# Decay attention followed by a mixture of experts: weight pieces loaded from the first chunk, splits at other places, reciprocals per expert

## The chip, the cores and the metric

The kernel runs on one core of one Trainium2 chip. The metric is device time in microseconds (us), lower is better. Engine names in the profile: PE is TensorE, DVE is VectorE, ACT is ScalarE, POOL is GpSimd, SP is the sync engine, which only asks for transfers here.

## The reference

```
# decay attention: q, k, v are (2, 8, 768, 64), lam is (8), blocks of 64
for b in range(nb):
    intra = einsum('bhic,bhjc->bhij', qb, kb) * Dmask        # Dmask[i,j] = lam ** (i-j) for i >= j
    intra = einsum('bhij,bhjd->bhid', intra, vb)
    inter = einsum('bhid,bhde->bhie', qb * lam_pow, kv_state)
    out[block b] = intra + inter
    kv_state = lam_block * kv_state + einsum('bhsd,bhse->bhde', kb * rev_pow, vb)
# mixture of experts on x = (1536 tokens, 512): 8 experts, hidden 1024, capacity 384 tokens
expert = argmax(x @ w_gate); gate = softmax(x @ w_gate)[expert]
out[token] = gate * (relu(x[token] @ w1[expert]) @ w2[expert])   # 0 past the capacity
```

All data are float32.

## The kernel before

**Attention.** The 1536 tokens are cut into 12 chunks of 128 (six to a batch entry). For each chunk s two loads of 512 KB come from memory: q and k transposed (tile qk, called load(s, 0)) and k and v by rows (tile kv, load(s, 1)); four buffers hold each kind. The work on a chunk is spread over several turns of one loop: score(s+2) and mask(s+2) run two turns ahead, attend(s) and state(s) in turn s, turn(s-1), choose(s-1), rows(s-1) and soft(s-1) one turn behind, place(s-2), placed(s-2) and scatter(s-2) two behind. score is q times k on PE (L412); mask multiplies by the decay on DVE (L419); attend forms x (L431, and L439 with the decayed qd and the state); state forms the new state (L465 on PE, L471 or L473 on DVE). decay_k and decay_q make kd (L395) and qd (L387) on POOL. turn multiplies x by an identity and the gate weights at once (tile tp, L482), which gives rows of tokens and gate logits. choose picks the expert on DVE (oh at L503 is the one-hot choice, cum at L507 the running count). soft makes the sum of exponentials on ACT, weight its reciprocal on DVE. place multiplies by a triangle on PE (L527, L528) for the rank of each token within its expert, placed takes it out on DVE (pr, L536), and scatter writes the 128 rows of the chunk to their places in xs, a table in device memory, with one indirect DMA that POOL issues (L553). Each row of xs is 512 values, the gate weight and the token's number. Before the first scatter, fill (L337) writes zeros into the places of experts 0 and 1 by two plain DMAs.

**Weights.** Every expert has 8 pieces of 128 x 1024 float32 (512 KB; four of w1, four of w2). load_w asks for a piece (tile wraw, four buffers), split_hi makes its high half on ACT (whi, L105), split_lo the remainder on DVE (wlo, L113), and all products of the experts are made of three products of such halves. In the loop, the tables LOAD, HI and LO say in which turn which piece is loaded and split.

**Experts.** Expert 0 gets its first 128 tokens while the last scatters run (class Solo, object first: turn, rest, up, cross, down, finish) and its next 128 in second. This stretch is called the transition here. Experts 1 to 7 follow in one loop of 232 places each (L770, L778, L796, L805). Rows of an expert are read back from xs (load_rows), tokens_of makes the token numbers, and put writes 128 rows of the result by an indirect DMA from POOL (L175). overflow is only run when an expert has more tokens than places.

**Order.** The schedule is written by hand: every engine runs its instructions in the order in which they stand in the program, and waits for other engines by semaphores. SP asks for all big loads and POOL issues the indirect DMAs, so a wait in one of these queues holds whatever stands behind it.

Of the kernel before, what the change touches and what calls it, by code (L numbers as in the profile page):

```python
# [8 lines left out]
F32 = mybir.dt.float32  # L9
# [28 lines left out]
LOAD = {3: (0,), 4: (1,), 5: (2,), 6: (3,), 7: (4,), 8: (5,), 9: (6,), 10: (7,), 11: (8,)}  # L38
HI = {5: (0,), 6: (1,), 7: (2,), 8: (3,), 9: (4,), 10: (5,), 11: (6,)}
LO = {6: (0,), 7: (1,), 8: (2,), 9: (3,), 10: (4,), 11: (5,)}  # L40
# [3 lines left out]
def kernel(  # L44
# [94 lines left out]
    rw, wt, ti = {}, {}, {}  # L139

    def load_rows(e, t=None):
        if e >= E:
            return
        if e > 0:
            rw[e] = rw_p.tile([P, RS // 32, P], F32, tag="rw", name="rw")
            wt[e] = ti_p.tile([P, NTT, 2], F32, tag="wt", name="wt")
            ti[e] = ti_p.tile([P, NTT], I32, tag="ti", name="ti")
            for q in range(4):
                i = nc.sync.dma_start(
                    out=rw[e][32 * q:32 * q + 32],  # L150
                    in_=xs[e * STR:e * STR + RS, P * q:P * q + P].rearrange("(t p) c -> p t c", p=32),
                )
                tc.add_to_no_dep_group("rows", i.ins)
# [5 lines left out]
        if t == 0:  # L159
            rw[e] = rw_p.tile([P, NTT, ROW], F32, tag="rw", name="rw")  # L160
            wt[e] = rw[e][:, :, DM:DM + 2]
            ti[e] = ti_p.tile([P, NTT], I32, tag="ti", name="ti")
        i = nc.sync.dma_start(out=rw[e][:, t], in_=xs[t * P:t * P + P])
        tc.add_to_no_dep_group("rows", i.ins)

    def tokens_of(e, t=None):
# [4 lines left out]
        )  # L171

# [8 lines left out]
    class Solo:  # L181
# [58 lines left out]
        def finish(self):  # L240
            y = self.sb("y")
            nc.scalar.activation(out=y, in_=self.y, func=AF.Copy, scale=wt[0][:, self.t, 0:1])
            put(y, 0, self.t)

    def attention():
        with ExitStack() as c2:
# [18 lines left out]
            nc.sync.dma_start(  # L265
# [115 lines left out]
            qd, kd, pt, tmp, xT, oneh, sc, stt, den, m8, tp, lg = ({} for _ in range(12))  # L381
# [127 lines left out]
            def soft(s):  # L509
# [5 lines left out]
                den[s] = sm.tile([P, 1], F32, tag="den", name="den")  # L515
                nc.scalar.activation(out=ex, in_=lg[s], func=AF.Exp, bias=nm, accum_out=den[s])

            def weight(s):
                if s < 0:
                    return  # L520
                nc.vector.tensor_scalar(out=den[s], in0=den[s], scalar1=1e-9, scalar2=None, op0=ALU.add)
                nc.vector.reciprocal(out=xg_all[:, s, DM:DM + 1], in_=den[s])
# [40 lines left out]
            mask(0)  # L563
            state(0)
            load(4, 0)
            fill()
            score(1)
            busy(4)
# [3 lines left out]
            mask(1)  # L572
            for s in range(NTILE):
                decay_k(s + 1)
# [3 lines left out]
                attend(s)  # L578
                if s > 0:
                    state(s)  # L580
                scatter(s - 2)
# [4 lines left out]
                if s == NTILE - 1:  # L586
                    first.turn()
                score(s + 2)
                mask(s + 2)
                weight(s - 1)  # L590
                if s == NTILE - 1:
                    first.rest()
                for i in LO.get(s, ()):
                    split_lo(i)
                for i in HI.get(s, ()):
                    split_hi(i)
                load(s + 6, 0)
                load(s + 4, 1)
                for i in LOAD.get(s, ()):
                    load_w(i)  # L600
                decay_q(s + 2)
# [4 lines left out]
            def tail(n):  # L606
                def go():
                    if n == 0:
# [4 lines left out]
                        weight(s)  # L613
# [29 lines left out]
            split_lo(6)  # L643
            split_hi(7)
            load_w(9)
            first.up(3, (None, count, None))
            split_lo(7)
            first.down(0)
            first.cross(1)
            split_hi(8)  # L650
            split_lo(8)
            load_w(10)
            load_w(11)
            split_hi(9)
            split_lo(9)
            load_w(12)
# [3 lines left out]
    def ffn(first):  # L660
        with ExitStack() as c2:
# [54 lines left out]
            load_w(13)  # L716
# [41 lines left out]
            for e in range(1, E):  # L758
# [43 lines left out]
                def finish(t):  # L802
                    m = min(P, SLOT - P * t)
                    y = y_p.tile([P, DM], F32, tag="y", name="y")
                    nc.scalar.activation(out=y[0:m], in_=yp[t][0:m], func=AF.Copy, scale=wt[e][0:m, t, 0:1])  # L805
                    put(y, e, t)

                def last(w2):
# [9 lines left out]
                    for c in range(2):  # L818
# [3 lines left out]
                        for p in range(4):  # L822
# [11 lines left out]
                            out=y[0:m, 0:cw], in_=ps[0:m, 0:cw], func=AF.Copy, scale=wt[e][0:m, 1, 0:1]  # L834
# [29 lines left out]
    def overflow():  # L864

        with ExitStack() as c2:
# [46 lines left out]
            for e in range(E):  # L913
# [5 lines left out]
                for o in range(ov[e]):  # L919
# [7 lines left out]
                    )  # L927
                    x = o2.tile([P, KD, 4, 32], F32, tag="ox", name="ox")
# [89 lines left out]
```

## Time and profile before

| | |
|---|---|
| median of 3 runs | 271.95 us (270.64 to 272.5) |
| profiled execution | 271.5 us, span of its instructions 269.8 us |
| PE busy | 241.7 us (90%) |
| DVE, ACT, POOL busy | 156.7, 131.1, 73.4 us |
| mean granted clock of PE | 0.976 of full speed |

The span goes from the first instruction to the last; times in the trace count from its start. An engine's busy share says little about what bounds a stretch: idle time ahead of an instruction is shown in brackets with what ended it, and that is inferred from semaphores, so a wait for several things is put down to the one that seems last.

### The profile page before, as it was taken

To read this page: it belongs to the slowest core of one execution; us is meant where nothing else is said; L and a number is where in the kernel's file an instruction comes from. 1 tells how busy PE (TensorE), PEld (TensorE's weight loads), DVE (VectorE), ACT (ScalarE), POOL (GpSimd) and SP (SyncE) were. 2 spreads that over 40 slices of the span, in tenths; PEclk is the share of its full clock that TensorE was granted. 3 is DMA by queue.
4 is the path that set the end of the run, shared out by engine and by line. 5 is a ranking of instruction groups with operands and counts; after the bars stand their busy time and mean duration, and the time that the engine had idled before them with its cause. 6 is when DMAs were issued, how large, how long until landed. Compare 5 with 4: busy or idle time off the path is not lost.

```text
span 269.8 us, 5296 instructions
## 1 busy us (share of the span) xinstructions
PE 241.7 (90%) x2046; PEld 209.4 (78%) x2046; DVE 156.7 (58%) x313; ACT 131.1 (49%) x227; POOL 73.4 (27%) x99
## 2 busy tenths in 40 slices
PE   6799986697788899999999999999999999999950
PEld 3688875485677678987997997897898799799850
DVE  5565655747566659688477567568657837702000
ACT  2054524755454567648455555566546646322110
POOL 6663657453230160100600500420140020020130
PEclk9999999869999999999999999999999999999995
DMA  6999899953335985997868759759839884020010
GB/s 133 409 327 331 280 311 414 412 194 129 128 148 153 336 236 192 291 316 259 271 144 328 253 149 320 250 181 318 272 135 285 285 258 157 2 69 0 4 60 5
DMA packets 27247, 58.97 MB, mean 219 GB/s; under 512 B 6274, under 2 KB 13444, under 8 KB 27216
## 3 DMA queue, kind: packets, MB, share of 16 engines
q1 hardware_dynamic: 23296, 51.41, 58.8%
q0 software_dynamic: 3216, 7.14, 7.1%
q8 instruction: 18, 0.29, 0.4%
q10 hardware_dynamic: 704, 0.02, 0.1%
q14 instruction: 13, 0.11, 0.1%
HBM read 50.37 MB, written 11.22 MB: 228 GB/s over the span
## 4 chain that ended last, share of the span: by engine, by line
issue 58%; PE 11%; POOL 11%; DMA 7%; DVE 6%; ACT 1%; SPq 1%; POOLq 1%; DVEq 0%
POOL out L175 5%; DMA wraw<-in_wp 4%; POOL xs L132 4%; PE tp L482 3%; PE sc L412 3%; DMA kv<-in_qkv 2%; PE st L465 2%; PE x L431 2%; DVE pt L419 2%; DVE wlo L113 2%; POOL xs L553 1%; SPq L262 1%; PE x L439 1%; POOL qd L387 0%; DVE cum L507 0%
## 5 line engine op out<-in xcount | busy, mean ns | idle before, releaser
L113 DVE TENSOR_TENSOR wlo<-wraw,whi 128x1024 fp32r<-128x1024 f32 x64 | 77.5, 1218 | 19.5 <-ACT whi L105 19.3
L105 ACT ACTIVATE whi<-wraw 128x1024 fp32r<-128x1024 f32 x64 | 66.6, 1051 | 24.0 <-DMA wraw<-in_wp 22.0
L770 PE MATMUL h<-xh,whi 128*128 128x232 f32 x224 | 61.6, 275 | 0.3 <-DVE hl L778 0.3
L770 PE MATMUL h<-xh,wlo 128*128 128x232 f32 x224 | 61.4, 274 | 0.0
L770 PE MATMUL h<-xl,whi 128*128 128x232 f32 x224 | 61.4, 274 | 0.0
L175 POOL DMA_INDIRECT out<-y,ti x13 | 14.0, 1079 | 119.9 <-ACT y L805 119.3
L770 PEld LDWEIGHTS h<-xh,whi 128*128 128x128 f32 x224 | 43.0, 192 | 1.0 <-DVE hl L778 0.5
L770 PEld LDWEIGHTS h<-xl,whi 128*128 128x128 f32 x224 | 42.9, 192 | 0.3
L770 PEld LDWEIGHTS h<-xh,wlo 128*128 128x128 f32 x224 | 42.9, 192 | 0.0
L796 PE MATMUL y<-whi,hh 128*128 128x512 f32 (+1 forms) x104 | 41.1, 395 | 0.0
L796 PE MATMUL y<-wlo,hh 128*128 128x512 f32 (+1 forms) x104 | 41.1, 395 | 0.0
L796 PE MATMUL y<-whi,hl 128*128 128x512 f32 (+1 forms) x104 | 40.9, 394 | 0.0
L778 DVE SCALAR_TENSOR_TENSOR hl<-h,hh 128x464 fp32r<-128x464 f32 x28 | 18.0, 641 | 38.5 <-ACT hh L777 38.5
L777 ACT ACTIVATE hh<-h 128x464 fp32r<-128x464 f32 x28 | 15.6, 558 | 37.6 <-PE h L770 37.6
L796 PEld LDWEIGHTS y<-whi,hl 128*128 128x128 f32 (+1 forms) x104 | 18.6, 179 | 5.6
L796 PEld LDWEIGHTS y<-wlo,hh 128*128 128x128 f32 (+1 forms) x104 | 18.6, 179 | 5.2
L796 PEld LDWEIGHTS y<-whi,hh 128*128 128x128 f32 (+1 forms) x104 | 18.6, 179 | 5.2
L419 DVE TENSOR_TENSOR pt<-sc,dt 128x512 f32<-128x512 f32 x24 | 15.4, 684 | 3.2 <-PE sc L412 3.1
L412 PE MATMUL sc<-qk 64*128 64x128 f32 x192 | 14.7, 295 | 1.1 <-DMA qk<-in_qkv 1.1
L805 ACT ACTIVATE y<-y,wt 128x512 f32<-128x512 f32 (+1 forms) x13 | 8.9, 686 | 13.4 <-PE y L796 12.8
L487 ACT ACTIVATE xg<-tp 128x512 f32<-128x512 f32 x12 | 7.2, 597 | 16.6 <-DVE l L495 16.5
L482 PE MATMUL tp<-iw,xT 128*128 128x136 f32 x96 | 15.2, 304 | 0.0
(117 smaller groups left out, 338.8 us busy)
## 6 DMA issues: line engine op xcount, KB each, us to landing
wraw<-in_wp SPq DMA_DIRECT2D x64, 512.0 KB, 4.6
qk<-in_qkv SPq DMA_DIRECT2D x12, 512.0 KB, 7.5
kv<-in_qkv SPq DMA_DIRECT2D x12, 512.0 KB, 8.4
rw<-xs SPq DMA_DIRECT2D x28, 128.0 KB, 3.5
xs<-zero SPq DMA_DIRECT2D x2, 514.0 KB, 12.4
rw<-xs SPq DMA_DIRECT2D x2, 257.0 KB, 2.8
out<-y,ti POOLq DMA_INDIRECT x13, 5.5
xs<-xg,slot POOLq DMA_INDIRECT x12, 5.6
```

The source lines that it names most:

```text
L105: nc.scalar.activation(out=hi, in_=raw[i], func=AF.Copy)
L113: nc.vector.tensor_tensor(out=lo, in0=t, in1=hi.bitcast(F32), op=ALU.subtract)
L132: i = nc.gpsimd.indirect_dma_start(out=xs, out_offset=bass.IndirectOffsetOnAxis(ap=padi[:, e, t:t + 1], axis=0), in_=zero, in_offset=None, ...
L175: i = nc.gpsimd.indirect_dma_start(out=out, out_offset=bass.IndirectOffsetOnAxis(ap=ti[e][0:m, t:t + 1], axis=0), in_=y[0:m], in_offset=No ...
L412: nc.tensor.matmul(sc[s][r][:, a], lhsT=kT[rs, a], rhs=qT[rs, a], start=True, stop=True)
L419: nc.vector.tensor_tensor(out=pt[s][:, r], in0=sc[s][r], in1=dt[:, r], op=ALU.mult)
L482: nc.tensor.matmul(tp[s][:, k, 0:P + E], lhsT=xT[s][:, k], rhs=iw[:, k], start=True, stop=True)
L770: nc.tensor.matmul(ps[:, f], lhsT=a[:, k, fs], rhs=b[:, k], start=(n == 0), stop=(n == 3 * KD - 1),)
L777: nc.scalar.activation(out=hh, in_=ps, func=AF.Relu)
L778: nc.vector.scalar_tensor_tensor(out=hl, in0=ps, scalar=0.0, in1=hh.bitcast(F32), op0=ALU.max, op1=ALU.subtract)
L796: nc.tensor.matmul(yp[t][0:m], lhsT=a[:, f, tsl], rhs=b[:, f], start=(p == 0 and f == 0 and n == 0), stop=(p == 3 and f == 1 and n == 2),)
L805: nc.scalar.activation(out=y[0:m], in_=yp[t][0:m], func=AF.Copy, scale=wt[e][0:m, t, 0:1])
```

## The change

Twelve pieces of weights are asked for in the loop, one a turn from turn 0 on; split_hi follows three turns and split_lo four turns later (before: load from turn 3 on, split_hi two and split_lo three turns later). Both stand at other places of a turn: split_lo behind placed, scatter and decay_k, split_hi behind attend and state. scatter(s-2) now stands ahead of decay_k(s+1). SP asks in the order kv, weight, qk instead of qk, kv, weight. attend(0) moves ahead of the loop. soft leaves the sum of exponentials in the row that is scattered, weight() goes, and the reciprocal is taken per expert in tokens_of (tile gt). The load of lam for the decay mask is issued by ACT instead of SP. At the end of the loop, first.turn and first.rest come one turn earlier, and the transition holds fewer splits and loads.

```diff
--- before.py
+++ after.py
@@ -35,9 +35,9 @@
 EARLY = 7
 FILLED = 2
 XO = 188
-LOAD = {3: (0,), 4: (1,), 5: (2,), 6: (3,), 7: (4,), 8: (5,), 9: (6,), 10: (7,), 11: (8,)}
-HI = {5: (0,), 6: (1,), 7: (2,), 8: (3,), 9: (4,), 10: (5,), 11: (6,)}
-LO = {6: (0,), 7: (1,), 8: (2,), 9: (3,), 10: (4,), 11: (5,)}
+LOAD = {s: s for s in range(12)}
+HI = {s: s - 3 for s in range(3, 12)}
+LO = {s: s - 4 for s in range(4, 12)}
 
 
 @with_exitstack
@@ -136,7 +136,7 @@
         apart(i, "xs", True)
 
     NTT = 2
-    rw, wt, ti = {}, {}, {}
+    rw, wt, ti, gt = {}, {}, {}, {}
 
     def load_rows(e, t=None):
         if e >= E:
@@ -145,6 +145,7 @@
             rw[e] = rw_p.tile([P, RS // 32, P], F32, tag="rw", name="rw")
             wt[e] = ti_p.tile([P, NTT, 2], F32, tag="wt", name="wt")
             ti[e] = ti_p.tile([P, NTT], I32, tag="ti", name="ti")
+            gt[e] = ti_p.tile([P, NTT], F32, tag="gt", name="gt")
             for q in range(4):
                 i = nc.sync.dma_start(
                     out=rw[e][32 * q:32 * q + 32],
@@ -160,6 +161,7 @@
             rw[e] = rw_p.tile([P, NTT, ROW], F32, tag="rw", name="rw")
             wt[e] = rw[e][:, :, DM:DM + 2]
             ti[e] = ti_p.tile([P, NTT], I32, tag="ti", name="ti")
+            gt[e] = ti_p.tile([P, NTT], F32, tag="gt", name="gt")
         i = nc.sync.dma_start(out=rw[e][:, t], in_=xs[t * P:t * P + P])
         tc.add_to_no_dep_group("rows", i.ins)
 
@@ -169,6 +171,10 @@
             out=ti[e][:, ts], in0=wt[e][:, ts, 1], scalar1=-1.0, scalar2=float(NT),
             op0=ALU.mult, op1=ALU.add,
         )
+        nc.vector.tensor_scalar(
+            out=gt[e][:, ts], in0=wt[e][:, ts, 0], scalar1=1e-9, scalar2=None, op0=ALU.add
+        )
+        nc.vector.reciprocal(out=gt[e][:, ts], in_=gt[e][:, ts])
 
     def put(y, e, t):
         m = min(P, SLOT - P * t) if e > 0 else P
@@ -239,7 +245,7 @@
 
         def finish(self):
             y = self.sb("y")
-            nc.scalar.activation(out=y, in_=self.y, func=AF.Copy, scale=wt[0][:, self.t, 0:1])
+            nc.scalar.activation(out=y, in_=self.y, func=AF.Copy, scale=gt[0][:, self.t:self.t + 1])
             put(y, 0, self.t)
 
     def attention():
@@ -262,7 +268,7 @@
                 nc.sync.dma_start(out=ld[s, half], in_=qkv[s // NC, s % NC, :, c])
 
             lam_sb = ac.tile([P, 2, HP], F32, name="lam_sb")
-            nc.sync.dma_start(
+            nc.scalar.dma_start(
                 out=lam_sb, in_=bass.AP(tensor=lam.tensor, offset=lam.offset, ap=[[0, P], [64 * (HP + 1), 2], [1, HP]])
             )
             for i in range(4):
@@ -378,7 +384,7 @@
             st = stb[:, 0:HP * D].rearrange("p (a d) -> p a d", a=HP)
             rank, early = (stb[:, DM // 2 + E * i:DM // 2 + E * i + E] for i in range(2))
 
-            qd, kd, pt, tmp, xT, oneh, sc, stt, den, m8, tp, lg = ({} for _ in range(12))
+            qd, kd, pt, tmp, xT, oneh, sc, stt, m8, tp, lg = ({} for _ in range(11))
 
             def decay_q(s):
                 if s >= NTILE or s % NC == 0:
@@ -512,14 +518,9 @@
                 nm = sm.tile([P, 1], F32, tag="nm", name="nm")
                 nc.scalar.activation(out=nm, in_=m8[s][:, 0:1], func=AF.Copy, scale=-1.0)
                 ex = sm.tile([P, E], F32, tag="ex", name="ex")
-                den[s] = sm.tile([P, 1], F32, tag="den", name="den")
-                nc.scalar.activation(out=ex, in_=lg[s], func=AF.Exp, bias=nm, accum_out=den[s])
-
-            def weight(s):
-                if s < 0:
-                    return
-                nc.vector.tensor_scalar(out=den[s], in0=den[s], scalar1=1e-9, scalar2=None, op0=ALU.add)
-                nc.vector.reciprocal(out=xg_all[:, s, DM:DM + 1], in_=den[s])
+                nc.scalar.activation(
+                    out=ex, in_=lg[s], func=AF.Exp, bias=nm, accum_out=xg_all[:, s, DM:DM + 1]
+                )
 
             def place(s):
                 if s < 0:
@@ -561,44 +562,44 @@
             decay_k(0)
             score(0)
             mask(0)
+            busy(2)
+            attend(0)
             state(0)
+            load(4, 1)
             load(4, 0)
             fill()
             score(1)
-            busy(4)
+            mask(1)
             decay_q(1)
             load(5, 0)
             tokens()
-            mask(1)
             for s in range(NTILE):
-                decay_k(s + 1)
                 place(s - 2)
                 carry(s)
                 placed(s - 2)
-                attend(s)
+                scatter(s - 2)
+                decay_k(s + 1)
+                if s in LO:
+                    split_lo(LO[s])
                 if s > 0:
+                    attend(s)
                     state(s)
-                scatter(s - 2)
+                if s in HI:
+                    split_hi(HI[s])
                 turn(s - 1)
                 choose(s - 1)
                 rows(s - 1)
                 soft(s - 1)
-                if s == NTILE - 1:
+                if s == NTILE - 2:
                     first.turn()
+                    first.rest()
                 score(s + 2)
                 mask(s + 2)
-                weight(s - 1)
-                if s == NTILE - 1:
-                    first.rest()
-                for i in LO.get(s, ()):
-                    split_lo(i)
-                for i in HI.get(s, ()):
-                    split_hi(i)
+                if s > 0:
+                    load(s + 4, 1)
+                load_w(LOAD[s])
+                decay_q(s + 2)
                 load(s + 6, 0)
-                load(s + 4, 1)
-                for i in LOAD.get(s, ()):
-                    load_w(i)
-                decay_q(s + 2)
                 if s == EARLY + 1:
                     load_rows(0, 0)
             s = NTILE - 1
@@ -610,7 +611,6 @@
                         choose(s)
                         rows(s)
                         soft(s)
-                        weight(s)
                     elif n == 1:
                         place(s - 1)
                         placed(s - 1)
@@ -640,20 +640,14 @@
             load_rows(1)
             first.up(2)
             first.cross(0)
-            split_lo(6)
-            split_hi(7)
-            load_w(9)
-            first.up(3, (None, count, None))
-            split_lo(7)
+            first.up(3, (count, None, None))
+            split_lo(8)
+            split_hi(9)
             first.down(0)
             first.cross(1)
-            split_hi(8)
-            split_lo(8)
-            load_w(10)
-            load_w(11)
-            split_hi(9)
+            load_w(12)
             split_lo(9)
-            load_w(12)
+            load_w(13)
             first.down(1)
         return first
 
@@ -713,7 +707,6 @@
                 ),
             )
             first.down(2)
-            load_w(13)
             second.turn()
             first.down(3)
             first.sb = room
@@ -802,7 +795,7 @@
                 def finish(t):
                     m = min(P, SLOT - P * t)
                     y = y_p.tile([P, DM], F32, tag="y", name="y")
-                    nc.scalar.activation(out=y[0:m], in_=yp[t][0:m], func=AF.Copy, scale=wt[e][0:m, t, 0:1])
+                    nc.scalar.activation(out=y[0:m], in_=yp[t][0:m], func=AF.Copy, scale=gt[e][0:m, t:t + 1])
                     put(y, e, t)
 
                 def last(w2):
@@ -831,7 +824,7 @@
                                     n += 1
                         y = y_p.tile([P, DM], F32, tag="y", name="y")
                         nc.scalar.activation(
-                            out=y[0:m, 0:cw], in_=ps[0:m, 0:cw], func=AF.Copy, scale=wt[e][0:m, 1, 0:1]
+                            out=y[0:m, 0:cw], in_=ps[0:m, 0:cw], func=AF.Copy, scale=gt[e][0:m, 1:2]
                         )
                         i = nc.gpsimd.indirect_dma_start(
                             out=half, out_offset=bass.IndirectOffsetOnAxis(ap=hi[0:m, c:c + 1], axis=0),
...
```

What is left out of the diff makes the same reciprocal in overflow, which these inputs do not reach.

## Rows read from the trace of the kernel before

**Rows 1.** Busy time by stretch; columns: stretch, us, busy of each engine (instructions), PEclk, DMA, GB/s.

```profile
50.00:60.00 10.00, 8.77 (x93) 7.36 (x92) 6.35 (x21) 5.56 (x17) 4.57 (x5) 0.66 0.72 277
...
130.00:150.00 20.00, 20.00 (x131) 17.48 (x131) 13.71 (x17) 11.58 (x15) 3.01 (x3) 1.00 0.76 246
```

**Rows 2.** Timeline of PE, the chunks; columns: start, us, instruction, count, idle before it.

```profile
23.30 1.10 PE L431 MATMUL x<-pt,kv 128*64 128x128 f32 x16
24.33 0.67 PE L439 MATMUL x<-qd,stt 64*64 64x128 f32 x16
25.03 0.69 PE L465 MATMUL st<-kv,kd 128*64 128x64 f32 x16
...
28.29 1.09 PE L431 MATMUL x<-pt,kv 128*64 128x128 f32 x16 [0.22 <-ACT ex L516]
...
43.16 1.09 PE L431 MATMUL x<-pt,kv 128*64 128x128 f32 x16 [1.19 <-ACT xT L444]
...
51.27 1.41 PE L431 MATMUL x<-pt,kv 128*64 128x128 f32 x16
...
59.12 1.09 PE L431 MATMUL x<-pt,kv 128*64 128x128 f32 x16
...
61.99 0.69 PE L465 MATMUL st<-kv,kd 128*64 128x64 f32 x16 [1.17 <-DVE pr L536]
...
70.95 1.09 PE L431 MATMUL x<-pt,kv 128*64 128x128 f32 x16
```

**Rows 3.** Timeline of PE, from the last chunk to expert 1.

```profile
70.83 0.17 PE L527 MATMUL st<-oh,upper 128*128 128x8 f16 x1 [0.96 <-DVE oh L503]
...
75.68 0.39 PE L211 MATMUL solo_ps<-whi,solo_xh 128*128 128x256 f32 x1 [0.76 <-ACT solo_xh L194]
...
84.42 0.47 PE L235 MATMUL solo_y<-whi,solo_hh 128*128 128x512 f32 x1 [1.18 <-DVE cnt L626]
...
92.11 0.38 PE L211 MATMUL solo_ps<-whi,solo_xh 128*128 128x256 f32 x1 [1.03 <-ACT solo_xh L194]
...
105.97 0.27 PE L770 MATMUL h<-xh,whi 128*128 128x232 f32 x1
```

**Rows 4.** Timeline of DVE in the chunks.

```profile
27.58 0.17 DVE L503 TENSOR_TENSOR oh<-iota_i,i 128x8 f16<-128x8 uint32 x1
...
36.43 0.63 DVE L503 TENSOR_TENSOR oh<-iota_i,i 128x8 f16<-128x8 uint32 x1
...
50.07 1.05 DVE L507 TENSOR_TENSOR cum<-cum,oh 128x8 f16<-128x8 f16 x1
...
59.09 1.29 DVE L419 TENSOR_TENSOR pt<-sc,dt 128x512 f32<-128x512 f32 x2 [0.75 <-PE sc L412]
...
60.55 1.21 DVE L113 TENSOR_TENSOR wlo<-wraw,whi 128x1024 fp32r<-128x1024 f32 x1
```

**Rows 5.** Timeline of POOL in the chunks.

```profile
24.48 1.20 POOL L553 DMA_INDIRECT xs<-xg,slot  x1 [4.04 <-ACT tmp L455]
25.71 1.29 POOL L387 TENSOR_TENSOR qd<-qk,qp 128x512 f32<-128x512 f32 x1
...
35.98 1.05 POOL L395 TENSOR_TENSOR kd<-kv,dt 128x512 f32<-128x512 f32 x1 [2.47 <-DMA kv<-in_qkv]
...
50.04 1.06 POOL L395 TENSOR_TENSOR kd<-kv,dt 128x512 f32<-128x512 f32 x1 [0.62 <-DMA kv<-in_qkv]
```

**Rows 6.** Timeline of ACT, two weight splits.

```profile
41.57 1.06 ACT L105 ACTIVATE whi<-wraw 128x1024 fp32r<-128x1024 f32 x1 [4.50 <-DMA wraw<-in_wp]
...
90.52 1.06 ACT L105 ACTIVATE whi<-wraw 128x1024 fp32r<-128x1024 f32 x1 [2.44 <-DMA wraw<-in_wp]
```

**Rows 7.** Timeline of SP, the issue of the fill.

```profile
10.25 0.89 SPq L337 DMA_DIRECT2D xs<-zero  x2
```

**Rows 8.** DMA issues with median us to landing; then the stretch from 40 to 50 us.

```profile
xs<-zero SPq DMA_DIRECT2D x2, 514.0 KB, 12.4
...
DMA packets 1148, 4.14 MB, mean 414 GB/s; under 512 B 142, under 2 KB 142, under 8 KB 1146
```

More of the change, by code (lines that the diff above doesn't have):

```diff
@@ L927, in overflow @@
                     )
+                    g = o2.tile([P, 1], F32, tag="og", name="og")
+                    nc.vector.tensor_scalar(
+                        out=g, in0=r[:, DM:DM + 1], scalar1=1e-9, scalar2=None, op0=ALU.add
+                    )
+                    nc.vector.reciprocal(out=g, in_=g)
                     x = o2.tile([P, KD, 4, 32], F32, tag="ox", name="ox")
@@ L952, in overflow @@
                     y = o2.tile([P, DM], F32, tag="oy", name="oy")
-                    nc.scalar.activation(out=y, in_=yp, func=AF.Copy, scale=r[:, DM:DM + 1])
+                    nc.scalar.activation(out=y, in_=yp, func=AF.Copy, scale=g)
                     nc.gpsimd.indirect_dma_start(
```

## The prediction

> **What bounds the kernel now.** I read the busy time by stretch first. From 106 us on, TensorE is busy in every microsecond (20.00 of 20 us) while VectorE has 13.71 of 20, and the DMA engines 0.76 [rows 1]; the first matmul of expert 1 starts at 105.97 us [rows 3]. From there on the end is fixed by matmuls alone: 269.8 less 106.0 is 163.8 us that this change doesn't touch. Whatever it does must show as an earlier 105.97. Next I read TensorE's timeline up to there. I write T(s) for the start of the matmuls of attend(s). T(3) is 23.30 and T(4) 28.29; without the 0.22 us of idle time ahead of it a full chunk takes 4.77 us with TensorE hardly waiting [rows 2]. From T(7) on, where every chunk carries weight splits too, it is slower: 8.11 us, then 7.85, and T(11) comes at 70.95 [rows 2]. From T(4) to T(11) that is 42.7 us, against 7 x 4.77 = 33.4 at the early pace. Three causes can be read. ScalarE stood 4.50 us on the load of the first weight piece, and everything behind that split in its queue with it [rows 6]. The subtraction for the low half (1.21 us) stands ahead of the rank product in VectorE's queue, and the state matmuls wait for that product, 1.17 us in chunk 9 [rows 2, 4]. And TensorE's clock fell to half for part of the stretch from 50 to 60 us (mean 0.66), just after such holes; chunk 8 lost 7.85 - 4.77 = 3.1 us, most of it by that [rows 1, 2]. Between T(11) and 105.97 lie 35.0 us, with holes of 0.76, 1.18 and 1.03 us that are named below [rows 3].
>
> **The change, part by part.** Times are in the profiled execution (span 269.8, own time 271.5, so 1.7 us around the span; the median of the runs is 271.95).
>
> *Start.* The lam load leaves SP, so the first q/k load goes out up to 0.5 us earlier; attend(0) moves ahead of score(1), and two warming matmuls go. mask(1) still has to end before score(2) gets its third PSUM buffer, and attend(1) stands behind score(2). I put 0 to -0.5 on all of it and take 0: the next step would swallow it.
>
> *The fill, which I expect to cost time.* scatter(0) writes into xs and must come after the two fills of xs. Its row names ScalarE as releaser, but that instruction is emitted later and cannot be it. The fill is issued at 10.25 and takes 12.4 us from issue to landing in the median [rows 7, 8], so it lands at about 23 to 24, and the scatter starts at 24.48 after 4.04 us of waiting [rows 5]. I read the wait as the fill's. In the kernel before, kd(3) is ahead of scatter(0) in POOL's queue, and only qd(4) is behind it (25.71). In the new order both kd(3) and qd(4) are behind it. The fill also gets one more 0.5 MB load ahead of it (kv of chunk 4; 0.524 MB at the 414 GB/s of rows 8 is 1.3 us) and starts some 0.4 us earlier through lam: the scatter starts at about 25.4. Then scatter 1.20, kd 1.06 [rows 5]: kd(3) is there at 27.7, where state(3) started at 25.03 [rows 2]. From state(3) to T(4) were 28.29 - 25.03 - 0.22 = 3.04 us, so T(4) comes at 30.8, 2.5 us **later** than before. If the fill doesn't hold the scatter, this is 0; if the fill lands 2 us later, 4.5.
>
> *Splits at other places.* The high half goes on ScalarE between the copy of x and the copy of the rows, the low half on VectorE between rank product and state update; both come three and four chunks after the load instead of two and three. The state matmuls then no longer wait for the low half (1.17 us), the wait on a load has a chunk more of cover, and the two small operations of weight() that stood ahead of the rank product go. So I expect the pace of 4.77 in chunks with splits too: chunk 4 4.77; chunk 5 has no state matmuls, 4.77 less 0.62 (25.03 less 24.33 is 0.70 for the part with qd, and the state part is alike); chunk 6 no part with qd, 4.77 - 0.70 [rows 2]; 7, 8, 9 4.77 each; chunk 10 has no score, but the rank matmul then waits for the choice, 0.96 us in the row, and takes the expert's transposes into that hole: again 4.77 [rows 3]. Sum 4.77 + 4.15 + 4.07 + 14.31 + 4.77 = 32.1.
>
> *What the move costs on VectorE and POOL.* oh takes 0.17 us alone; it took 0.63 when kd ran on POOL from 35.98 (both end at about 37.05), and cum 1.05 when kd ran from 50.04 [rows 4, 5]. So these operations stand still while POOL works on kd or qd. In the new order kd and qd stand together behind the scatter, in chunks 5 to 9, and that is about when oh and cum come. Per chunk this costs from 0 to kd and qd whole (1.06 + 1.29 = 2.35); I take 0.5, near the 0.46 of the row of oh: 2.5 us in five chunks. Then T(11) = 30.8 + 32.1 + 2.5 = 65.4, that is **5.5 us earlier** than 70.95.
>
> The Trainium skill's page "SBUF — State Buffer" (section "Who interferes with whom") has the rule: a VectorE instruction with two inputs in SBUF and a GpSimd instruction that reads SBUF exclude each other, and the second to come is blocked whole. The stretched rows agree. The low half of a split has two inputs in SBUF too, so by this rule it would also block, and be blocked; no row here shows that surely. That result is the third rival below.
>
> *Weights earlier.* One piece a chunk from the first, twelve by the end of the loop instead of nine. By kv(11) SP has asked for 24 loads and 7 pieces of 0.524 MB, 1.05 MB of fill and some 2.4 MB of scatters: 19.7 MB, at 414 GB/s 47.6 us, done by about 55 with a start at 5 and the slow fill. T(11) at 65 is behind that. The DMA would decide only below 19.7 / 60 = 330 GB/s. SP now asks for kv and the weight ahead of the q/k load, which waits for qd: kv no longer stands behind that wait.
>
> *The transition.* The first expert's transposes leave the end of the loop: its first product waited 0.76 us for xh, which is now ready. The low halves of pieces 6 and 7 leave VectorE's queue ahead of the copy of the counts, for which the down product waited 1.18 us. And piece 9, for which ScalarE stood 2.44 us with the second xh behind it, is loaded in the loop: 1.03 us of TensorE [rows 3, 6]. Sum **-2.97 us**, bounds -1.5 (one of the holes filled by the next wait) and -3.5.
>
> *Reciprocals.* Two small operations on VectorE per expert instead of per chunk, in a stretch where VectorE has 6 of 20 us free [rows 1]: nothing. Without that cover, 8 experts x 2 x some 0.17 (as oh) is 2.7 us.
>
> **Sum:** -5.5 - 3.0 = -8.5 on 271.5, that is 263.0 (263.4 from the median).
>
> **The rivals.** *One: the cover is better than I think.* No collisions (-2.5) gives 260.5; with no delay by the fill either, 258. For it speaks that the early chunks show oh at 0.17 while POOL does its share; against it the two stretched rows.
>
> *Two: the new hole lowers the clock.* While POOL waits for the fill, TensorE stands still for about 2.5 us, as long as the worst holes ahead of 51 us. If the clock falls as there, 3.1 us are lost: 266. For it speaks the 0.66 of rows 1; against it that there several holes followed one another.
>
> *Three, slower: VectorE and POOL take turns.* If the low half holds POOL, and POOL's products then hold oh and cum one after the other, a chunk becomes a chain of both engines: low half 1.21, scatter 1.20, kd 1.06, oh 0.17, qd 1.29, cum about 0.17, the masks 1.29 [rows 4, 5], 6.4 us, or 7.0 with slot, rank product and the gaps (an estimate). In chunks 5 to 9 that gives T(11) = 30.8 + 4.8 + 5 x 7.0 + 4.8 = 75.4 and with the transition 271.5 + 4.4 - 3.0 = 273; with the clock falling in the holes, 276. It decides from 6.7 us a chunk on. Against it: the scatter doesn't stretch such operations, and the operations must meet at the worst moment every time.
>
> *Four: the change doesn't shorten the waits on loads*, since the DMA is the limit already: 40 to 50 us ran at 414 GB/s. At 300 GB/s T(11) would be 5 + 66 = 71 and only the transition is gained: 268.5. Against it the stretch from 50 to 60 us, in which the DMA had 0.72.
>
> **How the numbers follow.** Forecast as summed, 260.5 to 265: 0.5. Rival one 0.22, rival two and half-way cases 0.12, rival four 0.06, rival three 0.10. A measurement of this kernel tells about 1% (2.7 us) from no change. The range runs from 257 (beyond rival one's 258) to 269 (rival four's 268.5); what lies outside is mostly rival three. Faster by over 1% (under 269.2) has 0.86, within 1% 0.08, slower 0.06.
>
> **What the changed profile would show.** Right: expert 1 starts at about 97; T(4) at 30 to 31 behind a kd(3) that ends at 27 to 28; the waits of the state matmuls on the rank product gone; chunks 5 to 9 at about 5 us with stretched oh or cum; no wait on wraw on ScalarE of over 1 us; the three holes of the transition gone; the stretch after expert 1's start as long as before. Wrong: if T(4) is at 28 or less, the reading of the fill falls; if chunks take 6 us or more with VectorE and POOL in turns, rival three holds; if a clock under 1.00 shows anywhere ahead of 60 us, rival two.

## The result, and the profile after

The changed kernel takes 275.26 us (median of 7 runs, 273.87 to 275.82) against 271.95 before: ratio 1.0149 [1.0112, 1.0185]. It is **slower**, by 1.5% and clear of no change; 263.0 was forecast. Medians here are of all runs, and the ratios with their 95% intervals leave out the few slow ones, in which the same kernel takes over 1.5% longer. Its profiled execution took 273.87 us, with a span of 272.1 (before 269.8), where the sum put 261.3. The 10.8 us between those two spans are what has to be found. First TensorE's timeline of the changed kernel: the starts of attend(0) and attend(1), then the rows with idle time ahead of them, then attend(4), attend(11) and expert 1 [rows 2, 3].

```profile
11.96 0.43 PE L437 MATMUL x<-pt,kv 128*64 128x128 f32 x2 [3.90 <-DVE pt L425]
...
18.65 1.09 PE L437 MATMUL x<-pt,kv 128*64 128x128 f32 x16
...
30.21 0.69 PE L471 MATMUL st<-kv,kd 128*64 128x64 f32 x16 [0.69 <-POOL kd L401]
...
35.20 0.17 PE L528 MATMUL st<-oh,upper 128*128 128x8 f16 x1 [2.09 <-DVE oh L509]
...
35.32 1.09 PE L437 MATMUL x<-pt,kv 128*64 128x128 f32 x16
...
46.08 0.17 PE L528 MATMUL st<-oh,upper 128*128 128x8 f16 x1 [2.26 <-DMA qk<-in_qkv]
...
58.70 0.17 PE L528 MATMUL st<-oh,upper 128*128 128x8 f16 x1 [1.66 <-DVE oh L509]
...
71.32 0.17 PE L528 MATMUL st<-oh,upper 128*128 128x8 f16 x1 [1.66 <-DVE oh L509]
...
75.95 1.09 PE L437 MATMUL x<-pt,kv 128*64 128x128 f32 x16
...
107.68 0.27 PE L763 MATMUL h<-xh,whi 128*128 128x232 f32 x1
```

The end was cut into four pieces by the prediction, and so it can be checked. T(4) is 35.32 where 30.8 was forecast: **+4.5**, all of it there since T(1), the start of attend(1), 18.65 against 13.98 before. From T(4) to T(11) it is 40.63 against 34.6: **+6.0**. From T(11) to expert 1 it is 31.73 against 32.05: -0.3. From there to the end it is 164.4 against 163.8: +0.6. Together 10.8. That last stretch is TensorE's alone, as before [rows 1]; busy time from 130 to 150 us:

```profile
130.00:150.00 20.00, 20.00 (x138) 17.84 (x137) 11.27 (x16) 9.22 (x12) 5.45 (x4) 1.00 0.69 227
```

The chain that ended last (columns: start, length, what) names the first two, the load of lam at the very start and oh in the chunks:

```profile
0.81 5.71 DMA lam_sb<-in_lam
...
43.47 2.57 DVE oh L509
...
56.69 1.97 DVE oh L509
...
63.17 1.80 DVE oh L509
...
69.31 1.97 DVE oh L509
```

The chunk from 66 to 72 us shows how it goes; VectorE first, then POOL [rows 4, 5]. (The first row of VectorE and the first two of POOL belong to the start: the scans that wait for lam, and scatter(0) with kd(3) behind it. They are used further down.)

```profile
6.62 1.69 DVE L310 TENSOR_TENSOR_SCAN dt<-lam_sb,anti 128x128 f32<-128x128 f32 x5 [5.14 <-DMA lam_sb<-in_lam]
...
66.28 0.15 DVE L537 SCALAR_TENSOR_TENSOR pr<-st,oh 128x8 f32<-128x8 f32 x1
...
66.36 1.22 DVE L113 TENSOR_TENSOR wlo<-wraw,whi 128x1024 fp32r<-128x1024 f32 x1
...
69.31 1.95 DVE L509 TENSOR_TENSOR oh<-iota_i,i 128x8 f16<-128x8 uint32 x1
71.30 0.16 DVE L513 TENSOR_TENSOR cum<-cum,oh 128x8 f16<-128x8 f16 x1
71.38 1.28 DVE L425 TENSOR_TENSOR pt<-sc,dt 128x512 f32<-128x512 f32 x2
72.58 0.15 DVE L537 SCALAR_TENSOR_TENSOR pr<-st,oh 128x8 f32<-128x8 f32 x1
```

```profile
27.85 1.20 POOL L554 DMA_INDIRECT xs<-xg,slot  x1 [3.00 <-ACT nm L519]
29.09 1.07 POOL L401 TENSOR_TENSOR kd<-kv,dt 128x512 f32<-128x512 f32 x1
...
66.50 1.12 POOL L553 CAST slot<-sraw 128x1 int32<-128x1 f32 x1 [1.57 <-DVE pr L537]
67.90 1.02 POOL L554 DMA_INDIRECT xs<-xg,slot  x1 [0.28 <-POOL slot L553]
68.94 1.07 POOL L401 TENSOR_TENSOR kd<-kv,dt 128x512 f32<-128x512 f32 x1
69.96 1.27 POOL L393 TENSOR_TENSOR qd<-qk,qp 128x512 f32<-128x512 f32 x1
```

Read the two side by side. The low half runs from 66.36 to 67.58, and the cast of the slot on POOL, 0.19 us alone, takes 1.12 and ends with it. The scatter and kd follow. oh comes at 69.31, while kd runs, and should have its turn when kd ends at 70.01; but qd starts at 69.96, and oh ends at 71.26, just after qd does (71.23). Then come cum, the masks, the next rank product, and the next low half. Summed along this chain (oh ends with qd, so it adds nothing): low half 1.22, gap 0.28, scatter 1.02, kd 1.07, qd 1.27, masks 1.28, rank product 0.15 = 6.3 us. The rank products are 6.30 us apart (66.28, 72.58). That is the third rival's chain, a little shorter than its 7.0. TensorE, which needs 4.6 us a chunk, waits for oh.

### The profile page after: what moved, and what is told of

The parts are those of the page before. It is cut to its first block, busy times and chain, and to the rows that moved or that the text cites. A ratio compares the mean times of both kernels' runs of the same rounds, so it can differ in the third digit from the quotient of the medians.

```text
span 272.1 us, 5290 instructions
## 1 busy us (share of the span) xinstructions
PE 242.3 (89%) x2044; PEld 210.4 (77%) x2044; DVE 165.7 (61%) x307; ACT 130.0 (48%) x227; POOL 83.2 (31%) x99
## 4 chain that ended last, share of the span: by engine, by line
issue 58%; POOL 13%; PE 11%; DVE 8%; DMA 6%; POOLq 1%; ACT 1%; SPq 0%; DVEq 0%
POOL xs L132 5%; DVE oh L509 4%; POOL out L181 4%; DMA xs<-zero 4%; PE tp L488 4%; PE x L437 3%; DMA lam_sb<-in_lam 2%; PE st L471 2%; PE x L445 2%; POOL xs L554 2%; DVE dt L310 1%; POOL kd L401 1%; DVE qp L318 1%; DVE i L507 1%; DVE l L501 1%
## 5 line engine op out<-in xcount | busy, mean ns | idle before, releaser
L105 ACT ACTIVATE whi<-wraw 128x1024 fp32r<-128x1024 f32 x64 | 66.5, 1050 | 25.4 <-DMA wraw<-in_wp 23.7
L181 POOL DMA_INDIRECT out<-y,ti x13 | 15.4, 1181 | 117.4 <-ACT y L798 115.9
L450 ACT ACTIVATE xT<-x 128x512 f32<-128x512 f32 x12 | 7.2, 597 | 30.1 <-PE x L445 18.4
L437 PE MATMUL x<-pt,kv 128*64 128x128 f32 x192 | 14.0, 284 | 4.1 <-DVE pt L425 4.1
L132 POOL DMA_INDIRECT xs<-zero,padi x12 | 14.3, 1192 | 3.7 <-issue 3.7
```

The lines of the kernel that those rows point to most:

```text
L105: nc.scalar.activation(out=hi, in_=raw[i], func=AF.Copy)
L132: i = nc.gpsimd.indirect_dma_start(out=xs, out_offset=bass.IndirectOffsetOnAxis(ap=padi[:, e, t:t + 1], axis=0), in_=zero, in_offset=None, ...
L181: i = nc.gpsimd.indirect_dma_start(out=out, out_offset=bass.IndirectOffsetOnAxis(ap=ti[e][0:m, t:t + 1], axis=0), in_=y[0:m], in_offset=No ...
L437: nc.tensor.matmul(at(a, r), lhsT=v[:, 2 * a + r], rhs=pt[s][:, r, a], start=(a < 2), stop=True, skip_group_check=True,)
```

## The experiments

"After" is the changed kernel. All ratios are to the kernel before, run beside it on the same chip.

**e1_lam_sp**: the load of lam back on SP, ahead of everything.

```diff
-            nc.scalar.dma_start(
+            nc.sync.dma_start(
                 out=lam_sb, ...
```

> The changed kernel with the lam load back on SP's queue, nothing else. Theory A (the lam load on ACT's queue lands some 3 us later, the decay mask and the first attend wait for it, and the delay of 4.7 us at attend(1) is passed on to the end): the decay scans start near 3.8 us instead of 6.6, attend(1) at about 14 instead of 18.65, T(11) some 4 to 5 us earlier, time 270.5. Rival (the delay at the start is absorbed by what follows, the fill or the loads): attend(1) earlier but T(11) within 1.5 us of 75.95, time 274 to 275.

Measured 272.31 us, 1.0019 [0.9984, 1.0053], span 269.3. lam now lands 3.0 us after its issue instead of 5.7; T(1) is 13.82, as expected. The time is 1.8 above the 270.5 that was expected, and T(11), at 73.11, is 2.8 us earlier and not 4 to 5. TensorE then, in e1's timeline:

```profile
27.36 1.11 PE L471 MATMUL st<-kv,kd 128*64 128x64 f32 x16 [2.66 <-POOL kd L401]
28.40 2.18 PE L488 MATMUL tp<-iw,xT 128*128 128x136 f32 x8
...
32.48 0.77 PE L437 MATMUL x<-pt,kv 128*64 128x128 f32 x10
```

The 4.8 us won at T(1) shrink to 2.8 at T(4), because now the fill holds: scatter(0) starts at 25.00, kd(3) at 26.24, and the state matmuls wait 2.66 us for it. Behind that hole the clock shows as well: the eight tp matmuls take 2.18 us where they take 1.19 at full clock. In the changed kernel the late lam had hidden most of this wait (0.69).

**x1_lam_head_start**: lam stays on ACT's queue; the other load of lam moves to the head of SP's, so that SP's first 512 KB load is asked for 0.43 us later.

```diff
+            lam_q = ac.tile([P, HP + 1], F32, name="lam_q")
+            nc.sync.dma_start(out=lam_q, in_=lam)
             lam_sb = ac.tile([P, 2, HP], F32, name="lam_sb")
             nc.scalar.dma_start(out=lam_sb, ...
```

> The changed kernel with the lam load for the mask still on ACT's queue, but the small load of the other lam table moved to the head of SP's queue, so that SP's first big load goes out half a us later than the lam load instead of at the same moment. Theory A (the lam load is slow because the 512 KB loads are asked for at the same moment and its small pieces stand behind theirs): the decay scans start at 3.8 to 4.5 us, attend(1) near 14, time 271 to 273 as with lam on SP. Rival (ACT's queue itself is slow for this load): scans at 6.6, time 274 to 276.

Measured 271.7, 1.003 [0.9993, 1.0066], like e1. The first row is VectorE's, the second SP's first big load:

```profile
3.92 2.63 DVE L310 TENSOR_TENSOR_SCAN dt<-lam_sb,anti 128x128 f32<-128x128 f32 x8 [2.44 <-DMA lam_sb<-in_lam]
```

```profile
1.24 0.42 SPq L268 DMA_DIRECT2D qk<-in_qkv  x1
```

The same load on the same queue, issued at 0.81 as in the changed kernel, is there at about 3.9. So it isn't ACT's queue that makes it late, but the first big load that is asked for in the same moment (SP at 0.81 in the changed kernel). The edit also takes the other load of lam from behind it on ACT's queue; that this one was the cause is unlikely by e1, where a load that was first on ACT's queue, with another issued 0.48 us behind it, took 3.1 us.

**e2_kd_first**: kd(s+1) back at the head of a turn, ahead of the scatter.

```diff
             for s in range(NTILE):
+                decay_k(s + 1)
                 place(s - 2)
...
                 scatter(s - 2)
-                decay_k(s + 1)
```

> The changed kernel with decay_k(s+1) back at the head of the turn, ahead of slot and scatter on POOL, as in the kernel before. Theory A (oh is shut out while POOL runs kd and qd one behind the other; on POOL's ring qd(s+2) is now followed by kd(s+2), so the pair stays): oh still takes 1.8 to 2.4 us in chunks 6 to 9, pace 6.0 to 6.3 us a chunk, time 274 to 276 (the wait of state(3) of 0.7 us goes). Rival (it is the new place of kd that costs): oh back near 0.2 to 0.6, pace about 5, time near 268.

Measured 269.16, 0.9889 [0.9802, 0.9976]. T(4) is 32.48 although lam is late (T(1) 18.71): kd(3) no longer stands behind the scatter. The time is near the rival's 268 and not theory A's 274 to 276, and yet the collisions stay, only with qd ahead of kd: oh up to 2.14 us, cum 1.88, and chunks 6, 7 and 8 take 8.0, 6.5 and 6.1 us. A row of VectorE, then two of POOL:

```profile
46.87 2.14 DVE L509 TENSOR_TENSOR oh<-iota_i,i 128x8 f16<-128x8 uint32 x1
```

```profile
46.69 1.28 POOL L393 TENSOR_TENSOR qd<-qk,qp 128x512 f32<-128x512 f32 x1
47.91 1.07 POOL L401 TENSOR_TENSOR kd<-kv,dt 128x512 f32<-128x512 f32 x1
```

Of the 5.2 us by which the span is shorter, 2.8 are won by T(4), where neither kd(3) nor oh is waited for any more, 1.5 from T(4) to T(11), and 0.9 behind it. So the place of kd behind the scatter isn't what makes the collisions, though it decides which chunks have them. The kernel before had the products in e2's order, but there kd stood waiting for kv most of the time [rows 5], 9.5 us over its ten instructions, 3.1 of it at the start; in e2 it is 0.8. I read it so, from the rows alone: kv asked for earlier brings kd right up behind qd, and that is enough.

**e3_products_first**: both products ahead of the scatter.

```diff
                 placed(s - 2)
-                scatter(s - 2)
                 decay_k(s + 1)
...
                     state(s)
+                decay_q(s + 2)
+                scatter(s - 2)
```

> The changed kernel with decay_k(s+1) and decay_q(s+2) both ahead of slot and scatter on POOL, so that they run beside the masks and the low half and POOL is in the scatter when oh and cum come. Theory A: oh at 0.17 to 0.5 us, pace 4.7 to 5.2 in chunks 6 to 9 (now 6.2), T(11) 6 to 9 us earlier, time 266 to 269. Rival (the exclusion only moves to the low half and the cast of slot): pace stays at 5.8 to 6.2, time 273 to 275.

Measured 266.95, 0.9828 [0.9767, 0.989], within theory A's range, but not by theory A's even pace. From T(8) to T(10) a chunk takes 4.59 us; chunks 6 and 7 take 7.3 each. In chunk 6 the low half itself was held (3.42 us at 43.03) and oh after it (1.54), and chunk 7 ran at half clock behind that hole (0.50 from 49 to 53 us). Order moves the collisions about; it doesn't end them.

**e4_psum**: order and queues as changed; the row of expert numbers, one input of oh, is kept in PSUM, and cum is formed from it instead of from oh, so that neither reads two tensors from SBUF.

```diff
+            nc.vector.tensor_copy(iota_p, iota_i)      # iota_p lies in PSUM
...
-                    out=oneh[s], in0=iota_i, in1=i8_all[:, s, 0:1].to_broadcast([P, E]), op=ALU.is_equal
+                    out=oneh[s], in0=iota_p, in1=i8_all[:, s, 0:1].to_broadcast([P, E]), op=ALU.is_equal
...
-                nc.vector.tensor_tensor(out=cum[s + 1], in0=cum[s], in1=oneh[s], op=ALU.add)
+                nc.vector.scalar_tensor_tensor(
+                    out=cum[s + 1], in0=iota_p, scalar=i8_all[:, s, 0:1], in1=cum[s], op0=ALU.is_equal, op1=ALU.add
+                )
```

> The changed kernel in which the list of expert numbers, one of the two inputs of oh and of cum, lies in PSUM instead of SBUF, so that both have only one tensor input in SBUF; POOL's order is untouched. Theory A (two inputs in SBUF are what POOL's products shut out): oh and cum take under 0.3 us beside kd and qd, pace 4.7 to 5.2, time 266 to 269. Rival (any small VectorE operation is held while POOL works on kd and qd, or POOL's queue itself sets the pace): oh still 1.8 us and more or the wait turns up elsewhere in the chunk, time 273 to 276.

Measured 263.58, 0.9745 [0.9667, 0.9822]: 11.7 us less than the changed kernel (10.4 in the spans of the profiled executions). The two groups of lines (line, instruction, count, then busy and mean ns) in the changed kernel and in e4:

```profile
L509 DVE TENSOR_TENSOR oh<-iota_i,i 128x8 f16<-128x8 uint32 x12 | 12.4, 1036 | 0.5
```

```profile
L514 DVE SCALAR_TENSOR_TENSOR cum<-st,i,cum 128x8 f16<-128x8 f32 x12 | 2.6, 217 | 0.0
L510 DVE TENSOR_TENSOR oh<-st,i 128x8 f16<-128x8 f32 x12 | 2.0, 167 | 0.4
...
L556 POOL CAST slot<-sraw 128x1 int32<-128x1 f32 x12 | 10.2, 852 | 8.5 <-DVE pr L540 8.3
```

oh falls from 1036 ns to 167. T(4) to T(11) is 32.3 us, where 32.1 was forecast without collisions, and no wait of the rank matmul on oh is left in it. The low half still holds the slot (852 ns in the mean) and costs nothing any more, since nothing on TensorE waits for it soon enough.

**b1_before_psum**: the same edit on the kernel before.

> The kernel before with the expert numbers in PSUM and nothing else, to see what the exclusion cost there. Its trace shows oh stretched by 0.46 and 0.36 us and cum by 0.89, together 1.7 us: expected a gain of 0 to 2 us, time 270 to 272. Rival (oh and cum in SBUF were a hidden cost of the whole loop there too): under 268.

Measured 268.33, 0.9917 [0.9874, 0.996]. That is near the rival's 268, below the 270 to 272 that was expected. So the kernel before (270.88 on that chip) paid some 2.5 us for the same exclusion; the change made it 10 to 12. In the trace it shows larger: T(4) to T(11) is 37.16 us where it was 42.66, for without the waits on oh and cum (1.33 and 0.89 us just ahead of 51) the clock doesn't fall either, 1.00 from 50 to 60 us where rows 1 have 0.66:

```profile
50.00:60.00 10.00, 7.72 (x126) 6.41 (x123) 6.87 (x26) 6.04 (x17) 5.27 (x8) 1.00 0.67 251
```

Against that this one execution of b1 has a T(4) 1.25 us later, with a clock of 0.72 from 8 to 14 us; whether its other runs have that too isn't known. What the prediction put down to the splits and their loads in the kernel before was thus in part oh and cum.

**c3_lam_psum, c4_lam_psum_fill, c2_lam_psum_kd**: e1 and e4 together; then, besides, the fill asked for ahead of load(4,·); or, instead of that, kd first as in e2.

```diff
+            fill()             # c4 alone
             load(4, 1)
             load(4, 0)
-            fill()
```

> The changed kernel with lam back on SP and the expert numbers in PSUM; kd stays behind the scatter. If the fill holds the first scatter and with it kd(3), as the prediction has it: the first scatter starts near 25, state(3) waits for kd(3) until 27.3 to 27.8, T(4) at 30.5 to 31, T(11) near 63, time 260 to 261.5. Rival (the fill costs nothing once oh is free): T(4) at 28, time as the run with decay_k moved back, 257 to 259.

> As the run before it (lam on SP, expert numbers in PSUM), and the fill is asked for ahead of the loads of chunk 4 instead of behind them, so that two loads of 0.5 MB (2.5 us at 414 GB/s) no longer stand ahead of it. If it is the fill's landing that the first scatter waits for: the scatter starts at 22.5 to 23, T(4) at 28 to 28.5, time 258 to 259.5. Rival (the scatter waits for something else): the scatter still starts at 25, time as without this edit.

> The changed kernel with three edits: lam back on SP, the expert numbers in PSUM (as in the run with PSUM alone), and decay_k(s+1) back at the head of the turn, so that kd(3) is not behind the scatter that waits for the fill. If the three costs are separate (late lam, POOL's products shutting out oh, fill ahead of kd(3)): attend(1) at 13.8, T(4) at 27.5 to 28.5, T(11) near 60.5, time 257 to 259. Rival (the loads become the bound once the rest is fast): T(11) not under 63 and weight splits or kd wait for loads by over 2 us, time 260 to 262.

Measured: c3 262.13, 0.9677 [0.9651, 0.9703]; c4 261.36, 0.9641 [0.9603, 0.9679]; c2 258.94, 0.9554 [0.9519, 0.959]. scatter(0) on POOL, then the state matmuls on PE, in c3; and scatter(0) in c4:

```profile
25.41 1.20 POOL L557 DMA_INDIRECT xs<-xg,slot  x1 [5.53 <-ACT xT L451]
```

```profile
27.77 1.12 PE L472 MATMUL st<-kv,kd 128*64 128x64 f32 x16 [3.08 <-POOL kd L402]
28.82 2.18 PE L489 MATMUL tp<-iw,xT 128*128 128x136 f32 x8
```

```profile
22.50 1.20 POOL L557 DMA_INDIRECT xs<-xg,slot  x1 [2.64 <-DMA xs<-zero]
```

The fill asked for 1.8 us earlier (9.83 instead of 11.66) moves scatter(0) 2.9 us forward, though POOL was ready at 19.9 in both: it is the fill that the scatter waits for, whatever the profile names (ACT's xT in c3). In c3 the clock is 0.83 from 20 to 40 us, and T(4) comes at 33.10, not at 30.5 to 31; T(11) is 65.55 and the time 0.6 above what was expected. In c4 the scatter starts when expected, but T(4) is 31.21, not 28 to 28.5, and the time 1.9 higher, for the load of q and k that the fill went ahead of is now late (score(5) waits 2.06). In c2, where kd(3) doesn't stand behind the scatter, the scatter still waits until 25.17, and T(4) is 27.69: the wait is there, and nobody needs it. c2 came out as expected in all four numbers (T(1) 13.72, T(11) 60.64).

**c5_old_weights**: c2 with the tables LOAD, HI and LO and the transition's splits and loads of the kernel before; the places of the splits within a turn stay new.

```diff
-LOAD = {s: s for s in range(12)}
-HI = {s: s - 3 for s in range(3, 12)}
-LO = {s: s - 4 for s in range(4, 12)}
+LOAD = {s: s - 3 for s in range(3, 12)}
+HI = {s: s - 5 for s in range(5, 12)}
+LO = {s: s - 6 for s in range(6, 12)}
```

> The fastest version so far (lam on SP, expert numbers in PSUM, decay_k at the head of the turn) with the old timetable of the weights: first piece in turn 3, splits two and three turns after, nine pieces in the loop, the transition's splits and loads as in the kernel before; the new places of the splits within a turn stay. If the earlier weights are worth what the prediction gave them (the holes of 1.18 and 1.03 us in the transition, and the wait of ACT on the first loads): time 2 to 5 us above the version with the new timetable, 261 to 264. Rival (with the chunks at full pace the early weights give nothing): within 1 us of it.

**c2_again** ran beside it.

> The fastest version once more, unchanged, on the chip of the run with the old timetable, for the difference between the two: 258 to 260, T(11) near 60.6.

Measured: c5 263.6, 0.9701 [0.9641, 0.9761]; c2 again 258.24, 0.9533 [0.9475, 0.9591]. T(4) is the same (27.59 and 27.69). ACT's first split in c5, then two rows of its PE:

```profile
38.79 1.06 ACT L105 ACTIVATE whi<-wraw 128x1024 fp32r<-128x1024 f32 x1 [4.17 <-DMA wraw<-in_wp]
```

```profile
40.39 1.19 PE L489 MATMUL tp<-iw,xT 128*128 128x136 f32 x8 [1.98 <-ACT xg L494]
...
75.65 0.47 PE L241 MATMUL solo_y<-whi,solo_hh 128*128 128x512 f32 x1 [1.17 <-DVE cnt L630]
```

The waits of before are back [rows 3, 6]. T(4) to T(11) takes 35.3 us against 32.95, and from there to expert 1 34.4 against 31.8. The weights from the first chunk on are worth about 5 us of c2's gain, half in the loop and half in the transition.

## Why the prediction was wrong

**What failed first: "What the move costs on VectorE and POOL".** I took 0.5 us a chunk, 2.5 in all, between 0 and 2.35. The trace shows waits of TensorE on oh between T(4) and T(10) of 2.26, 0.48, 1.66, 1.49 and 1.66 us, 7.55 together, and 2.09 ahead of T(4). (The row of the 2.26 names the load of qk; but oh ends at 46.04, and the matmul starts at 46.08. The 0.52 ahead of T(11) is left out: oh takes 0.17 there.) e4 takes the cause away and the stretch falls from 40.63 to 32.3, by 8.3. That is more than 7.55 because TensorE's clock fell behind the hole of 2.26, to 0.72 in the mean from 45 to 50 us, where the state and tp matmuls take 3.24 us for the usual 1.88:

```profile
45.00:50.00 5.00, 3.56 (x39) 3.21 (x39) 4.04 (x8) 1.54 (x2) 3.14 (x3) 0.72 1.03 404
```

It is less than both together, 8.9, mainly because e4 has a wait of its own, 0.76 us on the rows of the first expert. I had the mechanism, the ends of its price and the rival that would follow; what I got wrong was the choice of value. I took the row nearest to it (oh 0.63), where kd stood alone on POOL. With qd right behind kd, oh waited for both in five chunks. "The operations must meet at the worst moment every time" was my reason against rival three, and it was no reason: the chain keeps itself in step. oh's end releases the next rank product and low half, the low half holds the slot, and the slot starts the next kd and qd.

By the rule of the Trainium skill ("SBUF — State Buffer", "Who interferes with whom") a VectorE instruction with at most one SBUF input outside VectorE's 2-port modes doesn't contend with GpSimd, so the edit of e4 should have freed oh and cum; the trace agrees, 167 and 217 ns.

**What failed second: "Start".** I put the move of lam at 0 to -0.5 us. It cost 4.7 us at T(1). I looked for what left SP's queue and not at what the load would now run beside. VectorE's scans for the masks wait for it until 6.62 (3.76 before). That is 2.9 of the 4.7 us; 0.8 more is a scan of qp (the factors of qd) that now meets kd(0) on POOL (1.21 us instead of 0.40), and TensorE, idle for 3.9 us by then, has a clock of 0.68 from 12 to 15 us (1.00 before). SP's fourth load goes out later too (6.54, before 3.84), and so does the fill [rows 7]:

```profile
15.86 0.95 SPq L343 DMA_DIRECT2D xs<-zero  x2
```

e1 and x1 show the cause, each by another edit. By itself this step costs the changed kernel only 3.2 to 3.5 us (1.0149 to 1.003 or 1.0019), because the fill's wait comes out from behind it.

**The fill, right in kind.** kd(3) behind scatter(0) behind the fill: forecast were a scatter at 25.4 and kd(3) at 27.7. With lam in place they are at 25.41 and 27.77 (c3). T(4) then is at 33.10 instead of 30.8; the rest is the clock, rival two's, with 2.3 us where I had put 3.1. T(3) to T(4) is 7.50 us in the changed kernel, as forecast, but by accident: 0.69 for kd and 2.09 for oh took the place of the fill's 2.5.

**Splits and the pace: right.** The waits on the rank product are gone but for 0.36, no high half in the loop of the changed kernel waits for its load, and without the exclusion the pace is as summed (32.3; 32.95 in c2, of which 1.33 is a wait of the first expert's early transposes on the load of its rows; the sum had none).

**The transition: right.** -3.3 against -2.97; the holes of 0.76, 1.18 and 1.03 are gone [rows 3], and the largest that TensorE's timeline has between T(11) and expert 1 are 1.11 (a rank matmul, on an oh of 0.17 us, so no collision) and 0.77.

**Experts and reciprocals: as forecast, as far as can be told.** From expert 1 to the end it takes 164.4 us here, 163.75 in e4, 164.7 in c2, 164.2 in b1, which has the old reciprocals. The 0.6 can't be put down to them.

**DMA (rival four): not the limit.** c2 ran from 30 to 50 us at 409 to 411 GB/s; its splits wait 0.9 to 1.9 us for their loads, but TensorE keeps its pace but for the 1.33 us above.

Rival three gave 273 to 276; the measurement is 275.26, made up of its chain and of the late lam, which it didn't hold: that the number fits is luck in part. With lam back, both operations freed and kd first, the time is 258.94 and 258.24, where rival one's best case had 258. What stays open is how the 5 us or so between b1 (268.33) and c5 (263.6) divide among the places of the splits, the earlier transposes of the first expert and attend(0).

## What to carry to other kernels

Before placing GpSimd work next to VectorE work, list the VectorE operations on the critical path that read two tensors from SBUF and price each at up to the whole run of back-to-back GpSimd instructions that it can meet, not at one of them; moving one small operand into PSUM took 10 to 12 us off here, and 2.5 off the kernel before, at no cost that shows. A small load that everything waits for should be asked for some time ahead of the big ones (0.4 us was enough here), whatever queue it is in. When one delay is mended, look at which wait it had been covering: here 4.8 us at the start gave some 3 at the end, until the fill's wait was taken off the path too.

## What was not expected of the hardware

A VectorE operation that is held by one GpSimd instruction may have to wait for the next one too: five times in the changed kernel oh came shortly before kd or while it ran, and ended with qd (1.79 to 2.56 us). It isn't always so. In e3 the low half came at 38.87, while kd ran, and had its turn between kd and qd; qd was held instead. A row of VectorE, then two of POOL:

```profile
38.87 1.60 DVE L113 TENSOR_TENSOR wlo<-wraw,whi 128x1024 fp32r<-128x1024 f32 x1
```

```profile
38.34 1.05 POOL L401 TENSOR_TENSOR kd<-kv,dt 128x512 f32<-128x512 f32 x1 [1.52 <-DMA kv<-in_qkv]
39.35 2.25 POOL L393 TENSOR_TENSOR qd<-qk,qp 128x512 f32<-128x512 f32 x1
```

The same shows in c2 (low half from 51.57, ahead of a kd of 2.05 us), and in e2 cum from 41.01 ended with qd, though kd followed at once; another low half of e3, from 43.03, waited for both. What decides who is next is open. The cast of the slot, one value in each partition, took 1.12 us beside the low half instead of 0.19. The indirect scatter by itself didn't hold oh (0.17 us beside it in e2, at 36.81). But where a product followed the scatter at once, oh or cum that came in the scatter's last 0.2 to 0.5 us was held already (43.47 in the changed kernel, 41.01 in e2, 47.39 in e3); the rows don't tell whether the scatter's end or the product does it. The scatter itself took 1.65 us instead of 1.03 the one time in the changed kernel that it began during a low half (60.98, low half from 60.50), and 1.87 in c2 (29.10, low half from 28.85). A two-input operation on a single element (cum and short, 1x1) was held as well: 0.81 us in c2, where it met qd from 46.65, against 0.15. In the same kernel oh ran beside qd (31.00 to 32.27) at full speed, as VectorE's and POOL's rows of c2 show:

```profile
31.86 0.17 DVE L510 TENSOR_TENSOR oh<-st,i 128x8 f16<-128x8 f32 x1
...
47.15 0.81 DVE L551 TENSOR_TENSOR cum<-cum,short 1x1 f16<-1x1 f16 x1
```

```profile
31.00 1.27 POOL L394 TENSOR_TENSOR qd<-qk,qp 128x512 f32<-128x512 f32 x1
...
46.65 1.29 POOL L394 TENSOR_TENSOR qd<-qk,qp 128x512 f32<-128x512 f32 x1
```

And a load of 4 KB took 5.71 us from issue to landing when a 512 KB load was asked for in the same moment on another queue, and about 3.0 when it was ahead of it by 0.4 us or more.
